# An attention kernel whose order is planned at build time: merges start later, landings are planned longer, VectorE's blocks are chosen by readings left

## The chip, the cores and the metric

One core of one Trainium2 chip runs the whole program. The metric is the device time of one execution in microseconds, the median over runs. The engines are named as in the profile: PE (TensorE), ACT (ScalarE), DVE (VectorE), POOL (GpSimd), SP (SyncE, which issues most DMAs).

## The reference

The input x has 2048 rows of 640. Its layer norm feeds two branches, and x and both branches are added:

```python
q = (x @ wq).reshape(B, S, H, Dh).transpose(0, 2, 1, 3)      # H = 32 heads, Dh = 20
k = x @ wk                                                  # one key and one value head for all
v = x @ wv
scores = jnp.einsum("bhqd,bkd->bhqk", q, k) * (Dh ** -0.5)
p = _softmax(scores, axis=-1)
o = jnp.einsum("bhqk,bkd->bhqd", p, v)
A = o.transpose(0, 2, 1, 3).reshape(B, S, H * Dh) @ wo
B = silu(x @ w1) @ w2                                       # 640 -> 1728 -> 640
out = x_in + A + B
```

All arrays are bf16.

## The kernel before, in words

**Blocks.** The scores of one head for 512 queries and 128 keys are a block of 128 x 512 in one PSUM bank. Four chunks of 512 queries times 32 heads times 16 key tiles make 2048 blocks. Four heads of a chunk are a group (32 groups of 64 blocks, `GB`); each of the four sits in its own 32 rows of the PE array, so that a score step (`do_S`, line 1137) makes three or four blocks at once and a PV step (`do_pv`, line 978) multiplies up to four blocks, one per head, by V.

**Two ways through the exponential.** Most blocks go to ACT, which takes one, two or three banks in one instruction and writes E (line 1171). The others go to VectorE, which adds an offset to the scores and writes them as 16-bit integers into Z (line 1186); these bits, read as bf16, are a rough exponential. To make it finer, POOL adds two constants to the integers of a set of up to three blocks (a flush, `flush_z`), which gives two more copies in Y (line 1216, `INT64_ADD`), and PV reads all three with different weights of V: one *reading* of an ACT block, three of a VectorE block. Where `merge` holds, POOL adds other constants and issues a DMA that adds the second copy of Y onto the first (line 1221, `acc`); then PV reads Z and that sum, two readings. Merging needs a full set of three, less than `MG` us of planned backlog on POOL, and a distance from the group's end.

**Who takes a block.** `pick_dve` gives at most one block of a score step of three and two of a step of four to VectorE. It looks at VectorE's planned backlog against `DVE_TH` and `DVE_TH2`, and at `nz`, the count of VectorE's blocks of that head in that group: a head at `TILE_CAP` gets no more, and the head with the lowest count is taken first.

**The planner.** The program is written by a list scheduler that runs at build time (`Sched`, `Builder`). It keeps a clock per engine, gives each operation a planned duration and each result a time at which it is available, and puts on each engine what is ready with the lowest priority number. PE's order is made by `step`, which chooses among score steps, PV steps and jobs (projections, the silu branch, output rows). The chip then runs the five orders as written, each engine in its own order, with semaphore waits between them. A planned time that is too short shows on the chip as an engine that waits. For DMAs, `commit` plans the landing from the end of the issue, a rate per queue, and `op.late`. 29 tuning values of the planner stand in `SEG`, one row for every 32 score blocks.

**What else the change touches.** After a group, VectorE drains its sum (U, line 1269), an SP transpose turns it (line 1240, `uTd`, planned with `UT_LATE`), and VectorE takes the reciprocal (line 1255) and normalises (line 1260) into o. When a chunk's heads are all done, four transposes on SP turn o (line 1379, `oTd`), and the output jobs read that. Query projections of later groups are made by `qd_job` and copied into place by small DMAs on SP (line 1327). w1 is loaded after about 32 us, w2 and wo are loaded when the first group's sum is there (`late_loads`). Z has `NZ` slots of three blocks, Y has `NY` slots of two copies of three blocks; both are used in turn.

Of the kernel before, what the change touches and what calls it, by code (L numbers as in the profile page):

```python
# [35 lines left out]
UT_LATE = 2.0  # L36
UT_LATE1 = 4.0
# [12 lines left out]
ACC_ISSUE = 1.1  # L50
ACC_LAND = 4.0
MG = 3.0
MG_END = 16
# [5 lines left out]
NZ = 8  # L59
NY = 4  # L60
QS = 6
ZB = 3
# [45 lines left out]
GB = 4 * KT  # L108
# [125 lines left out]
class Sched:  # L234
    def __init__(self, nc, stack):
# [12 lines left out]
        self.lock_end = {"dve": 0.0, "pool": 0.0}  # L248
        self.busy = defaultdict(float)
        self.last_add = None  # L250
        self.dmaq = defaultdict(float)

    def sem(self, name):
        self.nsem += 1
# [1652 lines left out]
```

## Time and profile before

| | us |
|---|---|
| median of three runs | 691.84 (690.67, 691.84, 698.97) |
| profiled execution | 690.47 |
| its span, first to last instruction | 688.7 |
| PE busy | 656.0 (95%) |
| ACT busy | 651.3 (95%) |
| DVE busy | 609.4 (88%) |
| POOL busy | 516.7 (75%) |
| accumulating DMAs | 125 of 384 KB, median 4.2 from issue to landing |

The busy time of an engine is the time in which at least one of its instructions ran, so overlapping instructions count once. ACT's and PE's shares are means over stages: the first 30 us prepare inputs, the last 10 finish rows. A wait is listed as the waiting engine and line, an arrow, and who ended the wait, with the total, the number of times and the longest. PEld rows are weight loads, which run ahead of their matmuls.

### The profile page before, as it was taken

The numbers are of one execution on the slowest core, as the hardware profiler recorded it, in microseconds if no ns is written. First come the engines' busy times: TensorE is split into PE (matmuls) and PEld (weight loads), VectorE is DVE, ScalarE is ACT, GpSimd is POOL, SyncE is SP. The second block draws the span as 40 slices with busy tenths as digits, with TensorE's granted clock in tenths as the row PEclk, the third lists the DMA queues.
The fourth block names the chain that finished last, engine by engine and source line by source line (L and its number), as shares of the span: only waits on it lengthen the run. The fifth ranks groups of instructions, "written<-read, shape, count | busy, mean of one in ns | idle before, by whom it ended". The sixth has DMA issues, their size and how long they took to land.

```text
span 688.7 us, 22283 instructions
## 1 busy us (share of the span) xinstructions
PE 656.0 (95%) x9372; PEld 217.4 (32%) x9372; DVE 609.4 (88%) x1089; ACT 651.3 (95%) x748; POOL 516.7 (75%) x639
## 2 busy tenths in 40 slices
PE   8769999999998999999998999999999999999987
PEld 4312223333323333333233333233232323332323
DVE  7858899998897899998987987999998999899895
ACT  7959999999997999999998999999999999999995
POOL 2046768997886778987856988788878878778883
PEclk9979999999999999999999999999999999999999
DMA  7678833655455854545438665555434755641442
GB/s 204 131 219 167 208 78 61 101 110 101 94 109 110 175 104 88 96 79 85 85 71 140 125 144 115 110 102 107 97 77 89 152 130 101 107 80 32 79 78 63
DMA packets 69432, 75.86 MB, mean 110 GB/s; under 512 B 40566, under 2 KB 52694, under 8 KB 69334
## 3 DMA queue, kind: packets, MB, share of 16 engines
q0 software_dynamic: 18000, 49.16, 38.3%
q1 hardware_dynamic: 51190, 25.12, 16.0%
q8 instruction: 75, 1.23, 0.7%
q14 instruction: 23, 0.19, 0.1%
q10 hardware_dynamic: 144, 0.16, 0.1%
HBM read 11.44 MB, written 2.62 MB: 20 GB/s over the span
## 4 chain that ended last, share of the span: by engine, by line
PE 64%; DVE 16%; DMA 11%; POOL 4%; ACT 3%; issue 2%; SPq 0%; POOLq 0%
PE psall L978 24%; PE psall L1137 21%; PE psall L880 18%; DMA sbt<-sbt 10%; DVE sbt L1186 9%; POOL sbt L1216 4%; ACT sbt L1171 3%; DVE sbt L1260 2%; DVE sbt L1365 1%; DVE sbt L1659 1%; POOL sbt L1221 1%; DVE sbt L1269 1%; DMA sbt<-in_A_x_dram 1%; DVE sbt L1255 0%; PE psall L847 0%
## 5 line engine op out<-in xcount | busy, mean ns | idle before, releaser
L1171 ACT ACTIVATE sbt<-psall 128x1024 bf16<-128x1024 f32 (+2 forms) x660 | 620.9, 1073 | 26.1 <-PE psall L1137 25.3
L1216 POOL INT64_ADD sbt<-sbt x496 | 428.4, 959 | 129.7 <-DVE sbt L1186 104.2
L1186 DVE TENSOR_SCALAR sbt<-psall 128x512 uint16<-128x512 f32 x732 | 474.0, 682 | 54.0 <-PE psall L1137 46.3
L978 PE MATMUL psall<-sbt 128*32 128x512 bf16 x3137 | 252.4, 387 | 10.3 <-DMA sbt<-sbt 7.9
L1137 PE MATMUL psall<-sbt 32*128 32x512 bf16 x2048 | 250.9, 386 | 8.7 <-DVE sbt L1186 2.8
L880 PE MATMUL psall<-sbt 128*32 128x320 bf16 (+2 forms) x3923 | 228.6, 334 | 6.4 <-DMA sbt<-sbt 2.8
L1137 PEld LDWEIGHTS psall<-sbt 32*128 32x128 bf16 x2048 | 62.9, 91 | 246.9 <-ACT sbt L1171 163.5
L1221 POOL DMA_DIRECT2D sbt<-sbt x125 | 112.4, 899 | 31.2 <-POOL sbt L1216 28.1
L880 PEld LDWEIGHTS psall<-sbt 128*32 128x32 bf16 x3923 | 84.9, 96 | 93.3 <-issue 59.2
L978 PEld LDWEIGHTS psall<-sbt 128*32 128x32 bf16 x3137 | 60.6, 95 | 109.8 <-issue 71.3
L1365 DVE SCALAR_TENSOR_TENSOR sbt<-sbt,psall 128x512 bf16<-128x512 bf16 x54 | 36.8, 681 | 1.1 <-ACT sbt L1360 0.3
L1360 ACT ACTIVATE sbt<-psall 128x512 bf16<-128x512 f32 x54 | 37.1, 687 | 0.3 <-PE psall L880 0.3
L1260 DVE TENSOR_TENSOR sbt<-sbt 128x320 bf16<-128x320 bf16 x31 | 26.3, 849 | 0.1
L1269 DVE CAST sbt<-psall 128x512 bf16<-128x512 f32 x32 | 21.8, 680 | 4.3 <-PE psall L978 4.2
L1448 DVE SCALAR_TENSOR_TENSOR sbt<-psall,sbt 128x320 bf16<-128x320 f32 x28 | 13.3, 483 | 7.2 <-PE psall L880 7.1
L1429 DVE SCALAR_TENSOR_TENSOR sbt<-psall,sbt 128x320 bf16<-128x320 f32 x28 | 13.5, 482 | 0.5 <-PE psall L880 0.4
L1318 DVE TENSOR_SCALAR sbt<-psall 128x512 bf16<-128x512 f32 (+1 forms) x19 | 12.9, 679 | 0.3 <-PE psall L880 0.3
L856 PE MATMUL psall<-sbt 128*128 128x512 bf16 (+3 forms) x44 | 11.1, 408 | 1.2 <-DVE sbt L1614 1.2
L1659 DVE BATCH_NORM_STATS2 sbt<-sbt 128x6 f32<-128x320 bf16 x22 | 10.1, 473 | 1.3 <-DMA sbt<-in_A_x_dram 1.3
L1255 DVE RECIPROCAL sbt<-sbt 128x16 f32<-128x16 bf16 x31 | 7.6, 244 | 2.7 <-DMA sbt<-sbt 2.7
L1644 ACT ACTIVATE sbt<-sbt 128x640 bf16<-128x640 bf16 x5 | 3.6, 730 | 3.2 <-DMA sbt<-in_A_x_dram 3.2
L856 PEld LDWEIGHTS psall<-sbt 128*128 128x128 bf16 x44 | 4.4, 105 | 6.9 <-issue 1.9
(60 smaller groups left out, 82.8 us busy)
## 6 DMA issues: line engine op xcount, KB each, us to landing
sbt<-sbt POOLq DMA_DIRECT2D x125, 384.0 KB, 4.2
sbt<-in_A_x_dram SPq DMA_DIRECT2D x32, 160.0 KB, 3.6
out_dram<-sbt SPq DMA_DIRECT2D x15, 160.0 KB, 2.5
sbt<-in_B_w_dram SPq DMA_DIRECT2D x5, 432.0 KB, 5.8
sbt<-sbt SPq DMA_DIRECT2D x105, 20.0 KB
sbt<-in_B_w_dram SPq DMA_DIRECT2D x13, 160.0 KB, 5.2
sbt<-sbt SPq DMA_TRANSPOSE x58, 3.7
sbt<-in_A_wo_dram SPq DMA_DIRECT2D x5, 160.0 KB, 4.8
```

The lines of the kernel that those rows point to most:

```text
L880: ins = pe.matmul(self.bk(b, 0, n, r, r + SLOT), w[:, r:r + SLOT], x, start=start, stop=stop, tile_position=(0, r), skip_group_check=True)
L978: ins = pe.matmul(self.bk(ub[k], 0, QW, r, r + SLOT), self.v[:, it.w, it.kt, :], it.x(), start=f, stop=False, tile_position=(0, r), skip_g ...
L1137: ins = pe.matmul(self.bk(bank[x]), self.kT[r:r + SLOT, kt * P:(kt + 1) * P], self.qT[r:r + SLOT, g % QS, :], start=True, stop=True, tile_ ...
L1171: return a.activation(self.E[:, b0 * QW:(b0 + na) * QW].rearrange("p (b n) -> p b n", n=QW), src, AF.Exp, scale=ACT_SCALE)
L1186: return v.tensor_scalar(self.Z[:, zs, zp * QW:(zp + 1) * QW], self.bk(bb), OFF, ZMAX, ALU.add, ALU.min)
L1216: sc.new("pool", YP_FIX + YP_BLK * n, lambda g, k=k, sh=sh: g.int64_add(self.Y[:, ys, k, 0:w].bitcast(I64), self.Z[:, zs, 0:w].bitcast(I64 ...
L1221: op = sc.dma("pool", lambda g: g.dma_start(self.Y[:, ys, 0, 0:w].bitcast(BF16), self.Y[:, ys, 1, 0:w].bitcast(BF16), accum_op=ALU.add), [ ...
L1260: sc.new("dve", t_dve_ps(16 * DH), lambda v: v.tensor_tensor(dst, ut[:, :, :, 0:DH], rb, ALU.mult), [key, ("rL", up)], [("o", h0 + i) for ...
L1269: sc.new("dve", t_dve_ps(QW), lambda v: v.tensor_copy(self.U[:, up, :], self.bk(ub)), [("B", ub)], [("U", up)], prio=U_PRIO, name=f"Uev{g}")
L1360: sc.new("act", t_act(QW), lambda a: a.activation(t, src, AF.Tanh, scale=0.5), [("B", b)], [("tb", tp)], prio=TH_PRIO, name=f"th{c}_{fk}") ...
L1365: sc.new("dve", t_dve_ps(QW), lambda v: v.scalar_tensor_tensor(out=self.hT[0:rows, fk, :], in0=t, scalar=1.0, in1=src, op0=ALU.add, op1=AL ...
L1659: np_("dve", 0.41, lambda v, hf=hf: v.bn_stats(self.st6[:, n, hf, :], x[:, hf * 320:hf * 320 + 320]), self.xkeys(n), [("st6", n, hf)], pri ...
```

## The change

The planner gets other costs and another count; the program's operations keep their kinds and shapes.

- `merge` also needs the planner's PE clock to be past `ACC_FROM`, 78 us.
- An accumulating DMA is planned with 0.9 us of issue and 5.3 us from the issue's start to its landing (before: 1.1 and 5.1), and with 165 KB per us of its queue (before: 375). The three POOL operations behind one are planned 0.28, 0.22 and 0.12 us longer.
- U's transposes are planned 1.8 us later (the second one 1.0), and the query copies 1.8 us later past 78 us.
- A merged block takes half a count off its head's `nz`.
- Z has six slots and not eight, Y five and not four; together they take the same space.
- 60 of the 64 rows of `SEG` have other values. The mean of `TILE_CAP` goes from 6.75 to 6.91, of `MG` from 2.10 to 2.60, of `DVE_TH` from 6.06 to 5.25.

```diff
-UT_LATE = 2.0
-UT_LATE1 = 4.0
+UT_LATE = 3.8
+UT_LATE1 = 5.0
...
-ACC_ISSUE = 1.1
-ACC_LAND = 4.0
+ACC_ISSUE = 0.9
+ACC_LAND = 5.3
+ACC_RATE = 165e3
+ACC_NEXT = (0.28, 0.22, 0.12)
+ACC_FROM = 78.0
+ACC_DMA = 1.8
...
-NZ = 8
-NY = 4
+NZ = 6
+NY = 5
...
 SEG = (
-    (6.375, 0.382, 0.113, 0.226, 4, 5, 8, 0.66, 0.05, 4.33, 2.053, 34, 2.57, 1.281, 10, 6, 10, 54, 26, 33, 0, 0, 0, 2, 99, 0, 0, 1, 2),
+    (6.375, 0.295, 0.113, 0.226, 4, 5, 8, 0.66, 0.05, 4.33, 2.053, 34, 2.57, 1.281, 10, 6, 10, 54, 15, 33, 2, 0, 0, 3, 99, 0, 0, 1, 2),
...
@@ Sched.commit
+        if e == "pool":
+            if op.dma:
+                self.after_acc = 0
+            else:
+                if self.after_acc < len(ACC_NEXT):
+                    op.dur += ACC_NEXT[self.after_acc]
+                self.after_acc += 1
...
-                op.avail = max(op.end + 2.0, q + op.mode / 375e3) + op.late
+                op.avail = max(op.end + 2.0, q + op.mode / (ACC_RATE if op.name == "acc" else 375e3)) + op.late
@@ Builder.flush_z
-        merge = n == ZB and back < MG and self.bp < GB * (g1 + 1) - MG_END
+        merge = n == ZB and back < MG and sc.t["pe"] > ACC_FROM and self.bp < GB * (g1 + 1) - MG_END
...
             op.dur = ACC_ISSUE
-            op.late = ACC_LAND - 2.0
+            op.late = ACC_LAND - 2.0 - ACC_ISSUE
...
             self.merged += 1
+            for _, g, kt, j in self.zblocks:
+                self.nz[g][j] -= 0.5
@@ Builder.qd_job
                 ops[-1].dur = 0.74
+                ops[-1].late = ACC_DMA if sc.t["pe"] > ACC_FROM else 0.0
```

More of the change, by code (lines that the diff above doesn't have):

```diff
@@ L251, in __init__ @@
         self.dmaq = defaultdict(float)
+        self.after_acc = 99
     def sem(self, name):
```

118 rows, old and new, of the table SEG are left out of this document.

## The prediction

> **What bounds the kernel now.** I read the page first, then busy time by stage, then the waits, then the timeline around the longest gaps.
>
> ```profile
> span 688.7 us, 22283 instructions
> PE 656.0 (95%) x9372; PEld 217.4 (32%) x9372; DVE 609.4 (88%) x1089; ACT 651.3 (95%) x748; POOL 516.7 (75%) x639
> ...
> core 0: us, PE busy (x) PEld busy (x) DVE busy (x) ACT busy (x) POOL busy (x), PEclk, DMA share, GB/s
> 30.00:50.00 20.00, 13.96 (x159) 4.81 (x159) 10.91 (x24) 12.60 (x15) 7.96 (x10) 0.79 0.89 223
> ...
> 78.00:205.00 127.00, 127.00 (x1858) 40.57 (x1854) 116.92 (x198) 126.90 (x145) 105.81 (x129) 1.00 0.51 94
> 205.00:215.00 10.00, 7.61 (x96) 2.34 (x88) 5.69 (x10) 6.03 (x8) 4.41 (x6) 0.83 0.81 134
> 215.00:366.00 151.00, 149.68 (x2220) 48.72 (x2220) 137.81 (x231) 150.15 (x177) 120.78 (x149) 1.00 0.51 98
> 366.00:378.00 12.00, 9.57 (x141) 3.53 (x133) 8.40 (x15) 8.69 (x12) 6.42 (x8) 0.86 1.07 161
> 378.00:530.00 152.00, 148.78 (x2170) 47.52 (x2162) 139.98 (x232) 149.31 (x165) 126.60 (x154) 1.00 0.53 106
> 530.00:660.00 130.00, 125.58 (x1863) 41.60 (x1860) 120.72 (x205) 126.30 (x136) 106.03 (x129) 1.00 0.52 98
> ```
>
> The long stages are full: from 78 to 205 us ACT is busy 126.90 of 127 and PE all of it; from 215 to 366 ACT 150.15 of 151. There only less work helps. The lost time sits in short stages, where ACT's idle time is length less busy: 20 - 12.60 = 7.4 us in 30:50, 10 - 6.03 = 4.0 in 205:215, 12 - 8.69 = 3.3 in 366:378. In these the granted clock falls too (0.79, 0.83, 0.86).
>
> ```profile
> PEld psall L1137 <- ACT sbt L1171: 163.5, 418, 1.7
> PEld psall L1137 <- DVE sbt L1186: 46.4, 125, 0.8
> ACT sbt L1171 <- PE psall L1137: 25.3, 25, 6.4
> POOL sbt L1216 <- PE psall L978: 19.5, 17, 5.2
> PE psall L978 <- DMA sbt<-sbt: 7.9, 6, 5.3
> ...
> DVE sbt L1255 <- DMA sbt<-sbt: 2.7, 4, 1.0
> ```
>
> A score step (L1137) waits for a bank mostly until an exponential (L1171) has read it: 163.5 us, against 46.4 for VectorE's blocks (L1186). So ACT paces the steady stages, and ACT in its turn stands 25.3 us because PE stood. PE stands for landings: 7.9 us for readings (L978), of them 5.3 at once.
>
> ```profile
> 35.13 1.03 POOL L1221 DMA_DIRECT2D sbt<-sbt  x1 [0.32 <-POOL sbt L1216]
> ...
> 45.35 0.62 PE L978 MATMUL psall<-sbt 128*32 128x512 bf16 x4 [5.29 <-DMA sbt<-sbt]
> ...
> 46.56 1.02 ACT L1171 ACTIVATE sbt<-psall 128x1024 bf16<-128x1024 f32 x1 [6.41 <-PE psall L1137]
> ...
> L1221 POOL DMA_DIRECT2D sbt<-sbt x10: 877/877/1028, 35.1 to 85.2; - x10
> ...
> DMA to landing us min/median/max: 4.0/5.7/10.2
> ...
> L1221 POOL DMA_DIRECT2D sbt<-sbt x118: 852/877/1332, 79.5 to 672.8; - x118
> ...
>   PE psall L978: 2.4, 4
> ...
> DMA to landing us min/median/max: 3.8/4.2/6.5
> ```
>
> These are the timeline before 47 us, then line 1221 up to 86 us and from 78 us on. The accumulating DMA issued at 35.13 is read by a PV step that starts at 45.35, 10.2 us later, the longest landing of all; PE stood 5.29 us and ran this step of four in 0.62, where 0.40 is usual (row 212.60 below). Later the landings have a median of 4.2 and PE loses 2.4 us to them in all.
>
> **The change part by part.** Nearly all of it is in the planner, which writes the five engines' orders at build time. A planned duration costs the chip nothing; it moves instructions. The sum is made against the profiled execution, 690.47 us (span 688.7), which lies 1.4 under the median shown, 691.84.
>
> *No merges before 78 us on the planner's PE clock.* The plan knows no stall, and by then this trace has lost 7.4 us: 78 there is about 85 here, so the ten issues from 35.1 to 85.2 go. Without them the PV step at 45.35 waits for POOL's adds alone. I take the whole idle time of stage 30:50 as won: **-7.4 us**. Bounds: 5.3 (PE's gap alone) and 8.6 (with 28 - 26.80 = 1.2 of the next stage).
>
> ```profile
> 50.00:78.00 28.00, 27.18 (x361) 7.66 (x353) 24.10 (x38) 26.80 (x33) 18.14 (x24) 0.97 0.83 194
> ...
> 212.60 0.40 PE L978 MATMUL psall<-sbt 128*32 128x512 bf16 x4
> ...
> 213.25 0.83 PE L978 MATMUL psall<-sbt 128*32 128x512 bf16 x12
> ```
>
> Price: ten merges cover 30 blocks, which are then read three times and not twice, 30 readings. Four go in one step, and two more steps lengthen 0.40 to 0.83, so 0.215 each: 30 / 4 x 0.215 = **+1.6 us** of PE, taken in full because PE is full (nothing, if it lies in PE's 0.8 us of gaps there, to 1.6). POOL saves ten issues of 0.877, which nobody waits for.
>
> *Longer landings.* Planned from the issue's start, a merge was due after 1.1 + 2.0 + 2.0 = 5.1 us; now after 0.9 + 2.0 + 2.4 = 5.3, and when one follows close on another, 393 KB at 165 KB per us keep it 2.4 us behind. The 2.4 us of later waits sit at landings up to 6.5, probably of crowded issues, so I take **-2.4 us** (bounds 0 and -2.4; a dearer plan that puts readings off while PE has nothing else is a rival). [...]
>
> *U transposes later* (`UT_LATE` 2.0 to 3.8, so due 6.45 us after the start of their issue instead of 4.65).
>
> ```profile
> L1240 SPq DMA_TRANSPOSE sbt<-sbt x31: 1189/1249/2233, 56.7 to 663.0; - x31
> ...
> DMA to landing us min/median/max: 2.3/3.8/6.0
> ...
> L1255 DVE RECIPROCAL sbt<-sbt x31: 239/243/254, 61.7 to 666.7; 128x16 f32<-128x16 bf16 x31
> ...
>   PEld psall L1137: 1.4, 4
> ```
>
> The longest landing, 6.0, is now inside the plan. VectorE stood 2.7 us before the reciprocal, four times, with its blocks queued behind; score steps waited 1.4 us for that: **-1.4 us** (0 to -2.7). The later normalisation is wanted only by the next chunk's oT. Late q copies (`ACC_DMA`) get 0: no row shows a score step waiting for a copy; if the job's lead of 54 steps did not cover 1.8 us, it would cost 1.8 for each chunk.
>
> *Slots.* 496 adds are 248 flushes, one per 688.7 / 248 = 2.8 us.
>
> ```profile
> L1216 POOL INT64_ADD sbt<-sbt x496 | 428.4, 959 | 129.7 <-DVE sbt L1186 104.2
> L1186 DVE TENSOR_SCALAR sbt<-psall 128x512 uint16<-128x512 f32 x732 | 474.0, 682 | 54.0 <-PE psall L1137 46.3
> L978 PE MATMUL psall<-sbt 128*32 128x512 bf16 x3137 | 252.4, 387 | 10.3 <-DMA sbt<-sbt 7.9
> L1221 POOL DMA_DIRECT2D sbt<-sbt x125 | 112.4, 899 | 31.2 <-POOL sbt L1216 28.1
> ```
>
> A Y slot came round after 4 x 2.8 = 11 us and POOL waited 19.5 us for PV to free it; five give 14 us. POOL has 25% to spare, so this is worth 0 by itself and helps the term above. A Z slot came round after 22 us, now 17. VectorE never waited for one (its only releaser above is the score step), so 0; if six waited as the four Y slots did, up to 19.5 us of VectorE's queue, the drains and reciprocals behind it too. I stay at 0, because 17 us is longer than the five Y slots' 14.
>
> *Blocks by readings left.* ACT has 2048 - 732 = 1316 blocks, read once each; 125 merges of three leave 357 of the 732 unmerged: 1316 + 2 x 375 + 3 x 357 = 3137 readings, the count above. The head's cap (`TILE_CAP`, mean over the 64 rows of SEG 6.75, now 6.91) counted 732 / 128 = 5.7 blocks per head, near its commonest value, 6; with half a block off for each merged one the same choice counts (732 - 187.5) / 128 = 4.3. So the cap lets go, and VectorE's backlog limit decides (`DVE_TH`, mean 6.06, now 5.25). A block moved from ACT:
>
> ```profile
> 552.45 5.65 ACT L1171 ACTIVATE sbt<-psall 128x1024 bf16<-128x1024 f32 x6
> ...
> 458.08 1.02 ACT L1171 ACTIVATE sbt<-psall 128x1024 bf16<-128x1024 f32 x1 [0.80 <-PE psall L1137]
> ```
>
> Six exponentials of two blocks take 5.65, one 1.02, so (5.65 - 1.02) / 5 / 2 = 0.46 us of ACT a block; on VectorE it costs 474.0 / 732 = 0.65. Upper bound: VectorE's idle time between 78 and 660 us, 582 - 529.5 = 52.5, holds 81 blocks, -37 us. Lower: the lower `DVE_TH` takes 20 away, +9. I take 12 more, **-5.5 us**, nearer the low end, because VectorE is already 91% busy there and PE, as full as ACT, reads each added block once or twice more. Their 12 readings, 0.6 us, need four more merges to pay for them, and the merge limit `MG` rises from a mean of 2.10 to 2.60.
>
> *What stays.* PE's other long gaps:
>
> ```profile
> 208.38 1.18 PE L880 MATMUL psall<-sbt 128*32 128x320 bf16 x20 [2.39 <-issue]
> ...
> 372.87 1.53 PE L880 MATMUL psall<-sbt 128*32 128x320 bf16 x20 [2.43 <-DMA sbt<-sbt]
> ```
>
> These are output jobs at the start of a chunk, waiting for oT's transposes. Their planned cost is unchanged: 0, between -7.3 (both stages' 4.0 + 3.3 won by a luckier order) and +3.3 (one more).
>
> Sum: 690.5 - 7.4 + 1.6 - 2.4 - 1.4 - 5.5 = **675.4**; I say 675.
>
> **The rivals.** *B, only the early stall goes.* No blocks move and the longer landings merely change which wait is last: 690.5 - 7.4 + 1.6 = 684.7. For it: PE and ACT are both full, so a moved block shifts load between full engines. Against: VectorE and POOL have room.
>
> *C, the freed cap does more.* 40 blocks leave ACT, half of what VectorE holds: 40 x 0.46 = 18.4 instead of 5.5, so 675.4 - 12.9 = 662.5. For it: 5.7 of 6 says the cap bound nearly everywhere. Against: PE's extra readings.
>
> *D, slower: merges crowd.* `MG` goes up to 4 in many segments, so merges come in runs on the one POOL queue, land later than planned, and PE's in-order queue stands at a PV step with score steps behind it. One such gap of 2.4 us costs 4.0 with the slow clock after it (stage 205:215). The fourth cancels the gain of 15.1; eight, one in every fourth group of heads, give 675.4 + 32 = 707. For it: landings reached 10.2 while the queues were loaded. Against: that was beside weight loads, and with 118 issues later only four waits came of it.
>
> **How the numbers follow.** Forecast 0.50, own range 668 to 683; B 0.17; C 0.19; D 0.14. A measurement of this kernel can tell about 2% from no change, so faster means under 678.0 and slower over 705.7. Three quarters of the forecast's share lie under 678 (0.37) and all of C: 0.56. Within 2%: 0.13 of the forecast, B, 0.04 of D: 0.34. Slower: 0.10 of D. The range, 661 to 690, takes in C's and B's values and leaves out most of D and C's far end.
>
> **What would show it.** Right: no accumulating DMA before about 78 us, and ACT idle under 2 us from 30 to 50; PE's wait for readings under 2 us, the reciprocal's for its transpose under 1; 740 to 750 blocks at L1186's successor; ACT busy about 645. Wrong: the same or fewer such blocks (B), over 765 (C), or new PE gaps over 2 us before PV steps with landings over 6 us (D).

## The result, and the profile after

The kernel after takes 686.5 us (median of 20 runs, 679.8 to 696.1), the kernel before on the same chip 692.8 (20 runs, 687.8 to 700.2). Some executions are over 1.5% above the fastest of their kernel (8 of 20 after, 2 of 20 before); without these the medians are 684.3 and 692.5, and the ratio is 0.9882, with a 95% interval of 0.9852 to 0.9913. So the change gains 1.2%, 8.2 us, where 15.1 us were forecast. That is less than the 2% that the prediction asked for to call the kernel faster, but the interval leaves 1 out. In the numbers below the profiled execution after (span 684.6) stands against the one before (span 688.7).

The head of the page after, then busy time by stage in the columns known from before:

```profile
span 684.6 us, 22335 instructions
PE 659.6 (96%) x9402; PEld 215.5 (31%) x9402; DVE 626.2 (91%) x1101; ACT 646.7 (94%) x738; POOL 514.4 (75%) x639
```

```profile
core 0: us, PE busy (x) PEld busy (x) DVE busy (x) ACT busy (x) POOL busy (x), PEclk, DMA share, GB/s
30.00:50.00 20.00, 19.57 (x219) 6.50 (x217) 15.59 (x31) 17.68 (x22) 8.12 (x10) 0.82 0.61 184
...
78.00:205.00 127.00, 125.29 (x1840) 39.65 (x1837) 120.28 (x199) 125.59 (x141) 103.53 (x128) 1.00 0.48 86
205.00:215.00 10.00, 10.00 (x165) 3.47 (x161) 9.76 (x18) 9.89 (x11) 8.84 (x12) 1.00 0.73 132
215.00:366.00 151.00, 144.41 (x2068) 45.18 (x2066) 139.76 (x226) 141.07 (x159) 121.68 (x149) 0.98 0.53 104
366.00:378.00 12.00, 12.00 (x172) 3.46 (x165) 11.50 (x19) 12.00 (x16) 9.46 (x13) 1.00 1.10 132
378.00:530.00 152.00, 147.47 (x2177) 47.73 (x2173) 141.88 (x233) 145.34 (x163) 121.43 (x149) 0.99 0.52 97
```

The picture has turned over. The short stages that lost time before are full: ACT idles 20 - 17.68 = 2.3 us from 30 to 50 (7.4 before), 0.1 from 205 to 215 (4.0) and nothing from 366 to 378 (3.3). The long stages that were full now lose: 151 - 141.07 = 9.9 us from 215 to 366 (0.9 before) and 6.7 from 378 to 530 (2.7). Over the whole span ACT's idle time is 688.7 - 651.3 = 37.4 us before and 684.6 - 646.7 = 37.9 after. The span fell by 4.1 us and ACT's busy time by 4.6: what the early stalls gave was taken back in other places.

The list of waits after says by whom:

```profile
ACT sbt L1183 <- PE psall L1149: 24.1, 39, 2.5
POOL sbt L1228 <- PE psall L990: 10.8, 11, 1.8
...
PE psall L1149 <- DVE sbt L1198: 7.1, 7, 1.8
PE psall L892 <- DVE sbt L1198: 4.0, 2, 2.2
...
PE psall L1407 <- DVE sbt L1274: 1.5, 1, 1.5
...
PEld psall L990 <- DMA sbt<-sbt: 1.1, 4, 0.4
```

PE no longer waits for a reading (7.9 us before, only 1.1 of weight loads is left). It waits for VectorE's blocks (L1198) instead. VectorE itself is 91% busy, so the question is what it does just ahead of these waits. Its groups after:

```profile
L1198 DVE TENSOR_SCALAR sbt<-psall 128x512 uint16<-128x512 f32 x744 | 481.6, 683 | 39.9 <-PE psall L1149 31.8
L990 PE MATMUL psall<-sbt 128*32 128x512 bf16 x3185 | 251.8, 389 | 0.1
...
L1274 DVE TENSOR_TENSOR sbt<-sbt 128x320 bf16<-128x320 bf16 x31 | 36.7, 1184 | 0.0
```

and the instructions of the same normalisation before, with the shortest, median and longest in ns:

```profile
L1260 DVE TENSOR_TENSOR sbt<-sbt x31: 470/535/2791, 63.1 to 667.4; 128x320 bf16<-128x320 bf16 x31
```

The 744 blocks are the forecast 12 more. The third row is the surprise: the normalisation of a group, 31 instructions of one shape, has a mean of 1184 ns after, where 475 would do; before it was 26.3 / 31 = 849. Counted in the timelines, 7 of the 31 take over 1.0 us before and 12 after. Over 0.48 each they lose 26.3 - 31 x 0.48 = 11.4 us before and 36.7 - 14.9 = 21.8 after. Two places of the timeline after show what a long one does and what a short one looks like (start, duration, engine, instruction, count, idle time before it):

```profile
61.80 0.48 DVE L1274 TENSOR_TENSOR sbt<-sbt 128x320 bf16<-128x320 bf16 x1
61.98 1.78 POOL L1228 INT64_ADD sbt<-sbt  x2 [1.23 <-DVE sbt L1198]
...
304.87 3.06 POOL L1228 INT64_ADD sbt<-sbt  x3
...
305.84 2.44 DVE L1274 TENSOR_TENSOR sbt<-sbt 128x320 bf16<-128x320 bf16 x1
...
308.21 2.63 DVE L1198 TENSOR_SCALAR sbt<-psall 128x512 uint16<-128x512 f32 x4
308.94 0.83 PE L892 MATMUL psall<-sbt 128*32 128x512 bf16 x12 [1.80 <-DVE sbt L1198]
...
310.14 1.02 ACT L1183 ACTIVATE sbt<-psall 128x1024 bf16<-128x1024 f32 x1 [2.15 <-PE psall L1149]
...
310.67 0.61 PE L1149 MATMUL psall<-sbt 32*128 32x512 bf16 x3
```

At 61.80 the normalisation starts ahead of POOL's adds and takes 0.48 us. At 305.84 it starts while three adds run (304.87 to 307.93) and ends at 308.28, 0.35 after the last of them. VectorE's next block comes late, PE stands 1.80 us, ACT 2.15, and score steps of three then take 0.61 us instead of 0.39. Adding up PE's gaps over 0.15 us that begin in a normalisation or within 2.5 us behind it gives 7.6 us before and 15.5 after, where all of PE's gaps behind 30 us are 21.4 and 15.8. After, nearly all of PE's gaps are of this kind. In the kernel after, rows up to 0.95 us left no gap, rows of 1.6 to 2.0 left 0.7 to 1.0, rows of 2.4 to 2.85 left 1.5 to 2.2: what goes past about 0.9 us is handed on.

The gaps cost more than their length, because the granted clock fell behind four of them to 0.50 for 3.4 us each. This is the first such stretch, right behind the gap at 308.94, in the columns of the stages:

```profile
310.40:313.80 3.40, 3.40 (x34) 0.60 (x26) 2.36 (x4) 2.75 (x3) 2.43 (x4) 0.50 0.05 12
```

It is why the score step at 310.67 takes 0.61 us. By estimate, a stretch of 3.4 us at half the clock costs up to 3.4 x 0.50 = 1.7 us of PE. The four gaps were of 1.50 to 1.80 us; behind the longest of all, 2.21, the clock stayed at 1.00, so no limit can be read from these.

### The profile page after: what moved, and what is told of

Read it like the earlier page. It is cut to its first block, busy times and chain, and to the rows that moved or that the text cites. A ratio compares the mean times of both kernels' runs of the same rounds, so it can differ in the third digit from the quotient of the medians.

```text
span 684.6 us, 22335 instructions
## 1 busy us (share of the span) xinstructions
PE 659.6 (96%) x9402; PEld 215.5 (31%) x9402; DVE 626.2 (91%) x1101; ACT 646.7 (94%) x738; POOL 514.4 (75%) x639
## 4 chain that ended last, share of the span: by engine, by line
PE 58%; ACT 26%; DVE 14%; issue 1%; SPq 1%; DMA 1%; ACTq 0%
ACT sbt L1183 23%; PE psall L990 20%; PE psall L1149 20%; PE psall L892 16%; DVE sbt L1198 7%; DVE sbt L1274 4%; ACT sbt L1375 2%; DVE sbt L1380 1%; PE psall L1818 1%; DMA sbt<-in_A_x_dram 1%; SPq L1570 1%; DVE sbt L1332 1%; DVE sbt L1463 0%; DVE sbt L1269 0%; ACT sbt L1659 0%
## 5 line engine op out<-in xcount | busy, mean ns | idle before, releaser
L1183 ACT ACTIVATE sbt<-psall 128x1024 bf16<-128x1024 f32 (+2 forms) x650 | 617.2, 1093 | 24.8 <-PE psall L1149 24.1
L1228 POOL INT64_ADD sbt<-sbt x504 | 442.6, 951 | 140.7 <-DVE sbt L1198 127.1
L1198 DVE TENSOR_SCALAR sbt<-psall 128x512 uint16<-128x512 f32 x744 | 481.6, 683 | 39.9 <-PE psall L1149 31.8
L1149 PE MATMUL psall<-sbt 32*128 32x512 bf16 x2048 | 254.7, 389 | 13.4 <-DVE sbt L1198 7.1
L1233 POOL DMA_DIRECT2D sbt<-sbt x117 | 108.3, 926 | 14.2 <-POOL sbt L1228 13.3
L892 PEld LDWEIGHTS psall<-sbt 128*32 128x32 bf16 x3923 | 83.4, 95 | 92.7 <-issue 58.7
L990 PEld LDWEIGHTS psall<-sbt 128*32 128x32 bf16 x3185 | 59.7, 95 | 94.1 <-issue 69.5
L1380 DVE SCALAR_TENSOR_TENSOR sbt<-sbt,psall 128x512 bf16<-128x512 bf16 x54 | 36.7, 680 | 2.8 <-ACT sbt L1375 1.9
L1274 DVE TENSOR_TENSOR sbt<-sbt 128x320 bf16<-128x320 bf16 x31 | 36.7, 1184 | 0.0
L1283 DVE CAST sbt<-psall 128x512 bf16<-128x512 f32 x32 | 21.8, 680 | 4.2 <-PE psall L990 4.1
L868 PE MATMUL psall<-sbt 128*128 128x512 bf16 (+3 forms) x44 | 12.5, 443 | 1.2 <-DVE sbt L1629 1.2
L1818 PE MATMUL psall<-sbt 128*128 128x256 bf16 x40 | 7.3, 325 | 0.4 <-DVE sbt L1843 0.2
```

What stands on the lines that cost most here:

```text
L892: ins = pe.matmul(self.bk(b, 0, n, r, r + SLOT), w[:, r:r + SLOT], x, start=start, stop=stop, tile_position=(0, r), skip_group_check=True)
L990: ins = pe.matmul(self.bk(ub[k], 0, QW, r, r + SLOT), self.v[:, it.w, it.kt, :], it.x(), start=f, stop=False, tile_position=(0, r), skip_g ...
L1149: ins = pe.matmul(self.bk(bank[x]), self.kT[r:r + SLOT, kt * P:(kt + 1) * P], self.qT[r:r + SLOT, g % QS, :], start=True, stop=True, tile_ ...
L1183: return a.activation(self.E[:, b0 * QW:(b0 + na) * QW].rearrange("p (b n) -> p b n", n=QW), src, AF.Exp, scale=ACT_SCALE)
L1198: return v.tensor_scalar(self.Z[:, zs, zp * QW:(zp + 1) * QW], self.bk(bb), OFF, ZMAX, ALU.add, ALU.min)
L1228: sc.new("pool", YP_FIX + YP_BLK * n, lambda g, k=k, sh=sh: g.int64_add(self.Y[:, ys, k, 0:w].bitcast(I64), self.Z[:, zs, 0:w].bitcast(I64 ...
```

## The experiments

**Is it the normalisation beside the adds?** The theory: the normalisation, which reads two operands in SBUF, is held while POOL's adds run. The rival: the long rows are a symptom, and the adds, stretched and late, hold PE through Y. Four kernels take the contention out of each order, in two ways, and leave every order of instructions as it is.

`after_one` and `before_one` replace the multiplication by a copy that reads one operand and leave the division by the row sum out:

```diff
-v.tensor_tensor(dst, ut[:, :, :, 0:DH], rb, ALU.mult)
+v.tensor_reduce(dst, ut[:, :, :, 0:DH].rearrange("p q i (d x) -> p q i d x", x=1), AxisListType.X, ALU.add)
```

> The changed kernel with its order untouched; the normalisation (line 1274) is a copy with a single SBUF input and leaves the division by the row sum out. Theory 1, VectorE's normalisation is held by POOL's adds and hands its delay to the score steps: every one of its 31 instructions takes about 0.4 to 0.5 us instead of 0.48 to 2.85, PE's gaps behind it (15.5 us in all) vanish but for a microsecond or two, and the time falls by 10 to 16 us to 671 to 677, a ratio to the kernel before of 0.968 to 0.977. Rival, the long rows only show waits that the order has anyway: the rows get short and the time stays within 3 us of 686, ratio 0.985 to 0.992.

> The kernel before with the same replacement of the normalisation (line 1260), which leaves the division out. Theory 1: its gaps behind the normalisation are smaller (8.6 us on PE, 10.8 on ACT), so it gains 6 to 10 us, ratio 0.985 to 0.991, and the change is then worth 12 to 16 us between the two copies. Rival: no gain, ratio 0.997 to 1.003, and the change is worth the same 1.2% as before.

`after_next` and `before_next` keep the computation, and let POOL's next add wait until the normalisation is done, one wait for a group:

```diff
+yp = [o for o in order["pool"] if o.name[:2] == "yp"]        # POOL's adds
+for n in order["dve"]:
+    if n.name[:3] == "nrm":
+        for o in [o for o in yp if o.start > n.start][:1]:
+            o.deps.add(n)
```

> The changed kernel with its order untouched and one wait more for each normalisation: POOL's next add waits until the normalisation has ended. Theory 1: a normalisation is then held by the running add at most, its longest row falls from 2.85 to about 1.6 us, most of the 15.5 us of PE gaps go, POOL loses about 0.5 us for each of 31, which nobody waits for; time 673 to 679, ratio 0.971 to 0.980. Rival: POOL's delay makes Y late and PE waits for POOL or its DMAs instead, time 685 to 692.

> The kernel before with the same wait of POOL's next add for the normalisation. Theory 1: longest row from 2.79 to about 1.6 us, 5 to 8 us won, ratio 0.988 to 0.993. Rival: within 2 us of before, ratio 0.997 to 1.003, or slower, because the Y slots are only four and POOL has no time to give.

Measured (medians of 6 runs each), with before at 695.27 us beside them:

| | us | ratio to before, 95% |
|---|---|---|
| after_one | 665.19 | 0.9561 (0.9521 to 0.9600) |
| after_next | 664.90 | 0.9560 (0.9524 to 0.9596) |
| before_one | 682.74 | 0.9820 (0.978 to 0.986) |
| before_next | 685.77 | 0.9855 (0.9812 to 0.9897) |

`after_next`, its head, its waits and its groups:

```profile
span 661.6 us, 22332 instructions
PE 647.8 (98%) x9400; PEld 213.0 (32%) x9402; DVE 606.8 (92%) x1101; ACT 643.2 (97%) x738; POOL 513.2 (78%) x639
```

```profile
POOL sbt L1236 <- DVE sbt L1282: 19.9, 21, 1.7
...
ACT sbt L1191 <- PE psall L1157: 5.9, 17, 1.1
```

```profile
L1236 POOL INT64_ADD sbt<-sbt x504 | 438.8, 940 | 122.9 <-DVE sbt L1206 94.3 <-DVE sbt L1282 19.9 <-PE psall L998 4.8
...
L1282 DVE TENSOR_TENSOR sbt<-sbt 128x320 bf16<-128x320 bf16 x31 | 16.9, 547 | 0.0
```

The same multiplication, with the same two operands, now has a mean of 547 ns instead of 1184. POOL stands 19.9 us for it, which delays the adds; yet ACT's wait for PE falls from 24.1 to 5.9 us and the span by 23.0. Of these, 2.7 are won ahead of the first normalisation (it starts at 59.07 us, 61.80 in the kernel after), where the profiled execution after had a granted clock of 0.50 from 27.1 to 37.3 us and this one had not. The other 20 fit what is gone behind it: PE's gaps at normalisations fall from 15.5 to 0.6 us, and the four stretches at half clock, by the estimate up to 1.7 us each, with them (the mean clock of this profile is 1.00, of the one after 0.983). The adds come later at no cost, so the rival falls: it is VectorE's delay that counts. In `after_one`, where POOL waits for nothing new, the copy has a mean of 476 ns and the time is the same. The same two edits give the order before only 1.5 to 1.8%. Both kernels in the new order came out 6 to 8 us under what was expected of them, which counted PE's gaps and not the clock behind them.

So the change has two halves. With the contention out of both orders it is worth 0.9561 / 0.9820 = 0.974 (one operand) or 0.9560 / 0.9855 = 0.970 (POOL held); the two intervals, taken as independent, give about 0.006 on either side. It is 18 to 21 us, above the 15.1 forecast. The contention costs the order before 695.3 - 682.7 = 12.5 us or 695.3 - 685.8 = 9.5. For the order after it must be taken from ratios, because the kernel after was not run beside these: 0.9882 - 0.9560 = 0.032 of the time, some 22 us, of which up to 3 may be the early clock and not the contention. The difference, about 10 us, is what the forecast missed. `after_next` is the best kernel here: 4.4% under before, and 0.9560 / 0.9882 = 0.967 of the kernel after.

**How much delay is handed on, and the early stall.** `after_pad1` and `after_pad2` are `after_next` with one or two sums of VectorE ahead of each normalisation, each about 0.6 us (0.59 in the profile of `after_pad2`):

```diff
+for k in range(1):        # range(2) in after_pad2
+    v.tensor_reduce(self.pad[:, k:k+1], self.zero[:, :], AxisListType.X, ALU.add)
 v.tensor_tensor(dst, ut[:, :, :, 0:DH], rb, ALU.mult)
```

> The changed kernel with POOL's add held back behind each normalisation, and one sum over 512 elements of zeros put on VectorE right before each normalisation, about 0.6 us, 31 times; results are unchanged. Theory 1, what costs is VectorE's lateness at this place beyond what the order can absorb: in the changed kernel rows up to 0.95 us left no gap on PE and longer ones left their length less 0.9. So 0.5 + 0.6 = 1.1 us should cost about 0.2 us a group, 3 to 8 us in all: 667 to 673. Rival, what costs is that POOL's adds are stretched beside it and Y comes late: this pad has one SBUF input, POOL stays as fast as in the kernel without pad, and the time stays within 2 us of 665.

> The same with two such sums, about 1.2 us before each normalisation, 37 us of VectorE in all. Theory 1: 1.7 us at each group cost 0.7 to 0.8 each, 20 to 28 us in all: 685 to 693, as slow as the changed kernel or slower. Rival: within 5 us of 665.

Measured, with before at 694.28 beside them: 672.99 us, ratio 0.9667 (0.9613 to 0.9720), and 692.19, ratio 0.9967 (0.9930 to 1.0004). Both times are inside what theory 1 expected. `after_next`, without a sum, had 0.9560. From the page of `after_pad2`, from its timeline and from its waits:

```profile
PE 651.8 (94%) x9402; PEld 214.4 (31%) x9402; DVE 640.7 (93%) x1165; ACT 649.6 (94%) x738; POOL 512.1 (74%) x639
```

```profile
308.46 1.27 DVE L1286 TENSOR_REDUCE sbt<-sbt 128x1 f32<-128x512 bf16 x2
309.65 0.48 DVE L1287 TENSOR_TENSOR sbt<-sbt 128x320 bf16<-128x320 bf16 x1
```

```profile
POOL sbt L1237 <- DVE sbt L1287: 48.4, 24, 3.2
...
ACT sbt L1192 <- PE psall L1158: 25.6, 52, 1.4
...
PE psall L1158 <- DVE sbt L1207: 16.0, 24, 1.0
```

Two sums put the normalisation off by 309.65 - 308.46 = 1.19 us, 0.59 each. By the ratios the first of a pair costs 0.0107 of 694 us, 7.4 us or 0.23 for each of 32 normalisations, and the second 0.0300, 20.8 us or 0.65, all of itself. That is the bend seen in the gaps: by estimate from these numbers (0.59 - 0.23), VectorE can be late by about 0.4 us in this order on top of the normalisation's own 0.48, and hands on the rest in full. The profile of `after_pad2` has a granted clock of 1.00, so here the lateness alone cost 28 us, without a slower clock. POOL is held too, and longer; the kernels don't part that from VectorE's own delay, but 19.9 us of it cost nothing in `after_next`.

`before_w1` (on `before_next`) keeps the early merges and moves w1's loads behind the second merge's landing:

```diff
+first_w1_load.deps.add(acc[1])
```

> The kernel before with POOL's add held back behind each normalisation (0.9855 of before by itself), its order untouched, and one wait more: the five loads of w1, issued from 33 us on, wait for the second accumulating DMA to land. Theory: the early gap of PE (2.63 us there, 5.29 before) comes from the weight loads beside the first merge; that merge then lands in about 4.2 us and the gap goes, and 2 to 5 us are won, ratio 0.979 to 0.983, unless w1 comes late for its first job at about 57 us. Rival: the early merges are late for another reason (POOL's first DMAs, the transposes), and the gap stays over 2 us.

Measured: 686.33 us, ratio 0.9826 (0.9748 to 0.9905); `before_next` had 0.9855, inside that interval. The timeline (PE's rows alone) and the waits:

```profile
43.88 0.40 PE L900 MATMUL psall<-sbt 128*32 128x512 bf16 x4
44.10 0.60 PE L998 MATMUL psall<-sbt 128*32 128x512 bf16 x8
...
52.98 0.39 PE L1157 MATMUL psall<-sbt 32*128 32x512 bf16 x3
56.59 1.04 PE L900 MATMUL psall<-sbt 128*32 128x512 bf16 x6 [3.22 <-DMA sbt<-in_B_w_dram]
```

```profile
PE psall L900 <- DMA sbt<-in_B_w_dram: 3.2, 1, 3.2
PE psall L998 <- DMA sbt<-sbt: 2.7, 4, 0.8
```

The PV steps at 44 us stand for no merge any more, with the same merges in place. The first two merges land after 4.0 and 4.3 us, against 8.7 and 7.1 in `before_next`, and the two issued at 51.57 and 54.98, now beside the loads, after 8.6 and 8.5: it is the weight loads that make these landings long. But w1 is late by then, and a projection stands 3.2 us for it. The stall is moved, and no gain is shown; in the kernel after, where the merges start later, PE has no gap over 0.3 us between 38 and 60 us. The stall is also uncertain in size: PE's gap there is 5.29 us in the profiled execution before, but 2.63 in `before_next` and 1.16 in `before_one`, in the same order.

`after_early_next` is `after_next` with merges allowed from the start, and replanned:

```diff
-ACC_FROM = 78.0
+ACC_FROM = 0.0
```

> The changed kernel with POOL's add held back behind each normalisation, and merges allowed from the start again (ACC_FROM 78 to 0); the planner makes another order of it. Theory A, the gate is worth its stall: a PE gap of 1 to 5 us before a PV step near 40 us comes back, 666 to 672. Theory B, the 64 rows of tuning values were chosen for exactly these constants: any single one put back spoils the order in many places, 672 to 685, with little of the loss before 50 us.

Measured: 692.84 us, ratio 1.0003 (0.9960 to 1.0047), 28 more than `after_next` and more than either theory expected. The gap is back in its place in the timeline:

```profile
39.66 0.61 PE L998 MATMUL psall<-sbt 128*32 128x512 bf16 x8
45.09 0.62 PE L998 MATMUL psall<-sbt 128*32 128x512 bf16 x4 [4.81 <-DMA sbt<-sbt]
```

```profile
span 689.9 us, 22378 instructions
PE 667.6 (97%) x9426; PEld 223.6 (32%) x9426; DVE 608.0 (88%) x1100; ACT 649.0 (94%) x737; POOL 523.3 (76%) x655
```

That explains 5 us. ACT's idle time is 689.9 - 649.0 = 40.9 us against 661.6 - 643.2 = 18.4 and PE is busy 20 us longer: the planner makes another order everywhere behind the early one. That `SEG` was not chosen for it is a likely reason, but not shown. As a test of the early merges alone this run is inconclusive.

**Single constants.** Does one constant bring the long normalisations? `after_old_ut` puts `UT_LATE` back, `after_old_slots` the slots, and the other two do the reverse in the kernel before:

```diff
 after_old_ut:     -UT_LATE = 3.8; UT_LATE1 = 5.0   +UT_LATE = 2.0; UT_LATE1 = 4.0
 after_old_slots:  -NZ = 6; NY = 5                  +NZ = 8; NY = 4
 before_new_ut:    -UT_LATE = 2.0; UT_LATE1 = 4.0   +UT_LATE = 3.8; UT_LATE1 = 5.0
 before_new_slots: -NZ = 8; NY = 4                  +NZ = 6; NY = 5
```

> The changed kernel with the U transposes planned as before (3.8 to 2.0, 5.0 to 4.0); the planner makes another order. Read: how many of the 31 normalisations take over 1.0 us (7 before, 13 after). Theory 1, the later due time moves the normalisation into runs of POOL's adds: the count falls to 5 to 8, and the reciprocal waits for its transpose again, 1 to 4 us. Rival, it is where the order happens to put it: 9 to 15. In either case the tuning values no longer fit the constants and the time is 690 to 705.

> The changed kernel with eight Z and four Y slots. Theory 2, the fifth Y slot lets POOL run its adds without pause and so holds the normalisation longer: the count of those over 1.0 us falls to 5 to 8 and POOL's waits for PV rise from 10.8 to about 20 us. Rival, chance of the order: 9 to 15. Time 685 to 700.

> The kernel before with the U transposes planned late (2.0 to 3.8, 4.0 to 5.0) and nothing else. Theory 1: 11 to 15 normalisations over 1.0 us, the reciprocal's wait for its transpose (2.7 us) gone. Rival: 5 to 9. The time, with tuning values chosen for other constants, 695 to 715, slower than before.

> The kernel before with six Z and five Y slots and nothing else. Theory 2: 11 to 15 normalisations over 1.0 us, POOL's waits for PV fall from 19.5 to about 10 us. Rival: 5 to 9. VectorE should not wait for a Z slot by more than 3 us in all. Time 690 to 710.

(The texts count 13 long rows in the kernel after; there are 12.) Measured once each, with before at 692.35 beside them: 701.61, 690.45, 717.15 and 708.03 us. Normalisations over 1.0 us: 12, 12, 14 and 10. The groups of `after_old_slots`, then of `before_new_slots`:

```profile
L1228 POOL INT64_ADD sbt<-sbt x502 | 441.2, 965 | 153.8 <-DVE sbt L1198 102.3 <-PE psall L990 46.2 <-DVE sbt L1269 1.8
L1274 DVE TENSOR_TENSOR sbt<-sbt 128x320 bf16<-128x320 bf16 x31 | 36.6, 1182 | 0.2
```

```profile
L1216 POOL INT64_ADD sbt<-sbt x494 | 429.3, 966 | 135.6 <-DVE sbt L1186 128.3 <-PE psall L978 6.1
L1260 DVE TENSOR_TENSOR sbt<-sbt 128x320 bf16<-128x320 bf16 x31 | 28.9, 932 | 0.3
```

The slots do their own work: POOL waits for PV 46.2 us with four Y slots and 10.8 with five in the new order, 19.5 and 6.1 in the old one. The counts don't settle what brings the long rows. Put back in the new order, either constant leaves 12, as the rival said. Put into the old order, U's later transposes alone give 14, as theory 1 said, and the slots 10, between both. Three of the four times lie above all 20 runs of their base; 690.45 lies within those of the kernel after. Each constant makes another order, and each order was run once, so what a constant is worth, and why the new order puts more normalisations behind adds, stays open.

## Why the prediction was right and wrong

**Right.** The first merge is issued at 84.5 us (35.1 before). The merges' landings, planned longer, cost PE nothing, and the reciprocal's wait for U's transpose went from 2.7 to 0.0. VectorE took 12 more blocks, ACT's busy time fell by 4.6 us (5.5 forecast), merges went from 125 to 117 and readings from 3137 to 3185. Rival C (over 765 blocks) and rival D's mechanism (crowded merges) did not occur. B's 684.7 is close to the result by luck: its reason is wrong, as the blocks did move.

**The step that failed** is the clause that priced the moved normalisation at nothing: "The later normalisation is wanted only by the next chunk's oT." It asks who waits for its result. It does not ask what runs beside it on POOL, nor who stands behind it on VectorE: the blocks of the next score steps. The row was there before the change, 470/535/2791 ns for one shape and one size, and it was not read. Held normalisations cost 9.5 to 12.5 us then and some 22 now. These 10 us more cover the whole difference between the forecast gain, 15.1, and the measured one, 8.2; without them the change would have won 3 to 6 us more than forecast. The sum had no term for new stalls in the long stages, which it took as full: there ACT's idle time rose by 9.1 us from 215 to 366 and by 4.0 from 378 to 530. It is not shown that `UT_LATE` is what moved the rows beside the adds: with its old value the new order holds as many.

**Two terms were mis-sized and cancel in part.** The early stall was taken at 7.4 us from one execution. It came out as 5.1 of ACT's idle time, and the same order shows smaller gaps in `before_next` and `before_one`. "What stays" was set at 0, with the note that a luckier order might win both output jobs' gaps. That bound came true: these stages idle 0.1 us instead of 7.3, and `after_one` and `after_next` have no such wait either, while `before_one` and `before_w1` keep theirs. The landings of oT did not get shorter. The list of DMAs from issue to landing reads, before and after:

```profile
L1379 SPq DMA_TRANSPOSE sbt<-sbt x16: 1257/1574/3321, 202.5 to 642.4; - x16
...
DMA to landing us min/median/max: 2.4/5.1/7.2
```

```profile
L1394 SPq DMA_TRANSPOSE sbt<-sbt x16: 1181/1726/2463, 199.2 to 639.0; - x16
...
DMA to landing us min/median/max: 2.3/5.2/7.3
```

PE had other work at that time (10.00 of 10 us from 205 to 215). Why the new order put it there is not shown, so this gain is luck as far as the prediction goes.

**The list of signs** was met almost point for point (ACT idle 2.3 from 30 to 50 where under 2 was asked, 744 blocks, ACT 646.7), and the time was still 9 us over (684.3 against 675.4). None of the signs asked for the sum of ACT's idle time, which did not move.

## What to carry to other kernels

When a step is moved on an engine, ask what the neighbour engine runs beside it at its new place and who queues behind it, not only who reads its result. A group of one shape whose longest instruction is several times its shortest (470 and 2791 ns before) can hide a wait that the list of waits does not name: the normalisation has no row there as the one that waits. Where one engine's instructions hold back another's, as POOL's adds did the normalisation (1184 ns in the mean after, 547 in `after_next`), let the engine with time to spare wait: POOL was busy 75% of the span and VectorE 91%, and one wait per group on POOL was worth 3.3% in the new order, 1.5% in the old one.

## What the runs showed of the hardware

The normalisation, a VectorE instruction with two operands in SBUF, takes 0.48 us alone (179.37 in the kernel after), beside a DMA issue of POOL (239.88), and in the five rows where the first add beside it is recorded 0.18 us after its start (61.80 is one). It takes up to 2.85 us when adds run one after another from before its start (263.25), and took 1.64 and 1.65 at 197.53 and 219.39, where the add is recorded 0.14 and 0.15 us after its start; why these two differ from the five is not shown. At 305.84, by the recorded spans, it lasted past the ends of two adds and ended 0.35 us after the last of three. A copy with one operand took 468 to 486 ns in all 31 places of `after_one`.

The granted clock fell to 0.50 for 3.4 us behind PE gaps of 1.50, 1.60, 1.79 and 1.80 us in the kernel after, and was 1.00 behind the one of 2.21. In `after_pad2`, where PE waited 16.0 us for VectorE's blocks ahead of score steps and its longest wait of any kind was 1.3, the mean clock was 1.00.
